# An MM-DiT attention block on one core: the shift-times-V rows beside the text scale rows, and the text gate rows beside the text output, each as one tiled run, with the text adds on GpSimd

## Chip, cores, metric

One core of one Trainium2 chip. The metric is the device time of one execution in microseconds (us); medians of several runs are quoted. The "span" in a profile is from the first to the last instruction of one profiled execution, about 2 us less than the time. Runs carry a state, fast or slow; verdicts use fast runs.

## The reference

```python
B, Ni, Nt, D = (2, 256, 32, 1152)          # all bfloat16
mod_i = (silu(c) @ wmod_img).reshape(B, 6, 1, D);  mod_t = (silu(c) @ wmod_txt).reshape(B, 6, 1, D)
shi, sci, gai = mod_i[:, 0], mod_i[:, 1], mod_i[:, 2];  sht, sct, gat = mod_t[:, 0], mod_t[:, 1], mod_t[:, 2]
hi = layernorm(x_img) * (1 + sci) + shi;   ht = layernorm(x_txt) * (1 + sct) + sht
qkvi = hi @ wqkv_img;                      qkvt = ht @ wqkv_txt      # D -> 3D each
q, k, v = concat(text, image)              # 288 tokens per batch
a = softmax(q @ k.T * D**-0.5) @ v
out_i = x_img + gai * (a_img @ wo_img);    out_t = x_txt + gat * (a_txt @ wo_txt)
```

Nearly 40 MB of weights are read once each, in blocks of 1152 x 1152 (2.65 MB).

## The kernel before

Weights pass through five buffers ("slots"). A load into a slot is issued by SyncE, in program order, and can be issued only when everything that reads the slot's old weights is done:

```python
def load_w(slot, src, c0, splits=(D,)):        # one block into one slot, queue of SyncE
    t = wtile(slot)
    ...
        nc.sync.dma_start(t[:, :, o:o + n], sv[:, :, o:o + n])
...
w_k_i = load_w(4, wqkv_img, D)
w_sc_t = load_w(1, wmod_txt, D)
w_q_t = load_w(2, wqkv_txt, 0)
```

Small products with few rows run on "tiled" TensorE: four independent strips of 32 columns. These are the modulation rows (`gps` in the profile):

```python
def mod_rows_of(w, lhs):
    gps = ps_tr.tile([P, KT, LW], f32, tag="tr")
    for kt in range(KT):
        for g in range(NGG):                   # NGG = 4 strips
            mm(gps[LW * g:LW * g + LW], lhsT=lhs[:, kt, :], rhs=group(w, kt, g),
               start=(kt == 0), stop=(kt == KT - 1), tile_position=(0, LW * g))
    return gps
```

The image part does not apply the shift to its values directly: the product of shift and V weights is added later, as a row. For the text values that row has to be copied to 32 partitions, so it goes out to memory and is read back:

```python
def shift_v_rows():
    p_sv = mod_rows_of(w_v_i, shT32)
    nc.scalar.copy(svr[:], p_sv[:])
    cols["v"] = mod_cols_of(p_sv, "svc")
    for b in range(B):                         # the write, queue of ScalarE
        nc.scalar.dma_start(svd[b].rearrange("(c g l) -> g c l", g=NGG, l=LW), svr[b:P:LW])
    for g in range(2):                         # the read-back, queue of SyncE
        for b in range(B):
            r0 = 64 * g + NT * b
            nc.sync.dma_start(svb[r0:r0 + NT, :], svd[b, g * HD:(g + 1) * HD].partition_broadcast(NT))
...
v_last()
shift_v_rows()                                 # before the first q matmul
w_k_t = load_w(3, wqkv_txt, D)
w_ga_i = load_w(0, wmod_img, 2 * D)
w_v_t = load_w(1, wqkv_txt, 2 * D)
w_o_i = load_rows(4, wo_img, 0)
...
```

At the end the text gate takes a similar way through memory (`mod_scratch`, then `gbf`), and the text output stands after the third of four image tiles:

```python
out_img(0, C3)
out_img(1, C3, between=txt_gate)
out_img(2, C3)
out_txt()                                      # 64-column strips; product and add on VectorE
out_img(3, (CH, CH, 224, 160), parts=(2 * CH, D - 160, D))
```

Of the kernel before, what the change touches and what calls it, by code (L numbers as in the profile page):

```python
# [14 lines left out]
def kernel(  # L15
# [14 lines left out]
    nc = tc.nc  # L30
    bf = mybir.dt.bfloat16
    f32 = mybir.dt.float32
    PSUM = bass.MemoryType.PSUM

    B, NI, D = x_img.shape
    NT = x_txt.shape[1]
    P = 128
    KT = D // P
# [3 lines left out]
    NTT = B * NT  # L42
    CH = 384
    NCH = D // CH
    VC = 288
# [9 lines left out]
    ps_mm = ctx.enter_context(tc.tile_pool(name="ps_mm", bufs=6, space=PSUM))  # L55
    ps_tr = ctx.enter_context(tc.tile_pool(name="ps_tr", bufs=2, space=PSUM))

    pin = tc.keep_in_program_order

    def mm(*a, **k):  # L60
        return pin(nc.tensor.matmul(*a, **k))  # L61

    def tr(*a, **k):
        return pin(nc.tensor.transpose(*a, **k))  # L64
# [6 lines left out]
    x_i = act.tile([P, NIT, D], bf)  # L71
# [4 lines left out]
    def wtile(slot):  # L76
        return wpool.tile([P, KT, D], bf, tag="w%d" % slot, name="t")
# [6 lines left out]
    def load_w(slot, src, c0, splits=(D,)):  # L84
        t = wtile(slot)
        sv = wview(src, c0)
        o = 0
        for n in splits:
            nc.sync.dma_start(t[:, :, o:o + n], sv[:, :, o:o + n])
            o += n  # L90
        return t

    def load_rows(slot, src, c0, cuts=(0, 3, 6)):
        t = wtile(slot)
        sv = wview(src, c0)
        for r0, r1 in zip(cuts, cuts[1:] + (KT,)):
            nc.sync.dma_start(t[:, r0:r1, :], sv[:, r0:r1, :])
        return t
# [14 lines left out]
    w_sh_t = load_rows(0, wmod_txt, 0, (0, 1, 3, 6))  # L113
    nc.sync.dma_start(x_t[:], xt_flat[:, :])
    w_k_i = load_w(4, wqkv_img, D)
    w_sc_t = load_w(1, wmod_txt, D)
    w_q_t = load_w(2, wqkv_txt, 0)

    nc.scalar.preload_act_table_set("natural_log_exp_and_others")
    eps_t = eps_row[:, 0:1]  # L120
# [197 lines left out]
    t3, t0, t6 = [(x_tiles(k0, 1), k0, 1) for k0 in (3, 0, 6)]  # L318
# [63 lines left out]
    def qk_img(wq, blk, hooks):  # L382
        for j in range(KT):
            for hook in hooks.get(j, ()):
                hook()
            ps = ps_mm.tile([P, B * NI], f32, tag="mm")
            for kt in range(KT):
                mm(ps[:], lhsT=wq[:, kt, j * P:(j + 1) * P], rhs=hT_i[:, kt, :],
                   start=(kt == 0), stop=(kt == KT - 1))
            qk_evac(qkT[:, blk * KT + j, :, 0:NI], ps[:].rearrange("p (b n) -> p b n", b=B), blk)  # L390
# [4 lines left out]
    v_t = act.tile([P, HD + NTT], bf)  # L395
# [4 lines left out]
# [6 lines that stand above are left out]
        for g in range(2):  # L406
# [3 lines that stand above are left out]
# [84 lines left out]
    def qk_txt(blk, wq):  # L494
        for j0 in range(0, KT, FG):
            jn = min(FG, KT - j0)
            ps = ps_mm.tile([P, FG, NTT], f32, tag="mm")
            for j in range(j0, j0 + jn):
                for kt in range(KT):
                    mm(ps[:, j - j0, :], lhsT=wq[:, kt, j * P:(j + 1) * P], rhs=hT_t[:, kt, :],  # L500
                       start=(kt == 0), stop=(kt == KT - 1))
            qk_evac(qkT[:, blk * KT + j0:blk * KT + j0 + jn, :, NI:NTOK],
                    ps[:, 0:jn, :].rearrange("p j (b n) -> p j b n", b=B), blk)
# [11 lines left out]
    def v_txt_out(r, ps):  # L515
        pin(nc.vector.tensor_sub(v_t[:, r * VC:(r + 1) * VC], ps[:], svb[:, r * VC:(r + 1) * VC]))
        if r == 0:
            pin(nc.vector.tensor_sub(v_t[0:NTT, HD:HD + NTT], ps[NTT:P, 0:NTT], svb[NTT:P, 0:NTT]))
# [20 lines left out]
    gb = act.tile([P, B, D], bf, tag="Bt")  # L539
    gbf = act.tile([P, 2, VC], bf)  # L540
    xf = act.tile([P, 2, VC], bf)
# [14 lines left out]
    def txt_gate():  # L556
        mod_row_out(mod_rows(w_ga_t), 1)
        for g in range(2):
            for b in range(B):
                r0 = 64 * g + 32 * b  # L560
                nc.gpsimd.dma_start(gbf[r0:r0 + NT, :, :],
                                    gsc[1, b, :].rearrange("(r g j) -> g r j", r=2, g=2)[g].partition_broadcast(NT))

    v_last()
    shift_v_rows()
    w_k_t = load_w(3, wqkv_txt, D)
    w_ga_i = load_w(0, wmod_img, 2 * D)
    w_v_t = load_w(1, wqkv_txt, 2 * D)
    w_o_i = load_rows(4, wo_img, 0)
    w_ga_t = load_w(3, wmod_txt, 2 * D)  # L570
    w_o_t = load_rows(1, wo_txt, 0, (0, 5))
    qk_img(w_q_i, 0, {0: (shift_part(0, 2),), 3: (txt_stats, shift_part(2, 4), txt_var, txt_norm),
                      5: (shift_part(4, 7),), 8: (shift_part(7, KT),)})
    qk_img(w_k_i, 1, {1: (txt_transposes,), 4: (txt_rows_scale, shift_blocks, txt_scale),
                      7: (shift_fold, txt_shift), 8: (lambda: qk_txt(0, w_q_t),)})
    qk_txt(1, w_k_t)

    aT = act.tile([P, KT, B * NTOK], bf, tag="Q")
    qpos = [[0, P, 2 * P], [NT, NT + P, 0]]
# [50 lines left out]
    def p_transposes(kj, pool):  # L630
        ps = pool.tile([P, B * NTOK], bf, tag="tr" if pool is ps_tr else "mm", name="pT_ps")
        k0 = kj * P
        for pb, c0, o in [(pbs[(0, qi)], k0, qpos[0][qi]) for qi in range(TPB)] + [(pbs["t"], k0, NI)] + \
                [(pbs[(1, qi)], k0 - (NT if kj == 2 else 0), NTOK + qpos[1][qi]) for qi in range(TPB)]:
            tr(ps[:, o:o + P], pb[:, c0:c0 + P], ident[:])
        return ps

    def p_out(kj, ps, copy, b0=0, b1=B):
        pin(copy(pT[:, kj, b0 * NTOK:b1 * NTOK], ps[:, b0 * NTOK:b1 * NTOK]))
# [55 lines left out]
    v_txt_out(0, vt[0])  # L695
    vt.append(v_txt(1))
    pt0, pt1, pt2 = p_transposes(0, ps_tr), p_transposes(1, ps_tr), p_transposes(2, ps_mm)
    v_txt_out(1, vt[1])
    p_out(0, pt0, nc.scalar.copy, 0, 1)
    p_out(0, pt0, nc.vector.tensor_copy, 1, B)  # L700
    p_out(1, pt1, nc.scalar.copy, 0, 1)
    p_out(2, pt2, nc.vector.tensor_copy)
    p_out(1, pt1, nc.scalar.copy, 1, B)
    img_gate_spread()
    for dts in ((0, 5, 1), (6, 2, 7), (3, 8, 4)):
        attn_pair(*[[(b, dt) for dt in dts] for b in range(B)])

    def out_img(i, chunks, parts=None, between=None):
        b = i // TPB
        t0 = b * NTOK + qpos[b][i % TPB]  # L710
        o = work.tile([P, D], bf, tag="o")
        c0 = s0 = 0
        for n in chunks:
            if c0 and between:
                between = between()
            ps = ps_mm.tile([P, CH], f32, tag="mm")
            for dt in range(KT):
                mm(ps[:, 0:n], lhsT=aT[:, dt, t0:t0 + P], rhs=w_o_i[:, dt, c0:c0 + n],
                   start=(dt == 0), stop=(dt == KT - 1))
            tmp = work.tile([P, CH], bf, tag="tmp")  # L720
            nc.vector.tensor_mul(tmp[:, 0:n], ps[:, 0:n], gb[:, b, c0:c0 + n])  # L721
            nc.vector.tensor_add(o[:, c0:c0 + n], tmp[:, 0:n], x_i[:, i, c0:c0 + n])  # L722
            c0 += n
            if parts is None and c0 == D or parts and c0 in parts:
                (nc.scalar if parts and c0 == D else nc.sync).dma_start(oi_v[b, i % TPB, :, s0:c0], o[:, s0:c0])
                s0 = c0

    def out_txt():
        of = work.tile([P, 2, VC], bf, tag="of", bufs=1)
        for r in range(2):  # L730
            ps = ps_mm.tile([P, VC], f32, tag="mm")
            for dt in range(KT):
                for g in range(2):
                    c0 = (2 * r + g) * VC
                    mm(ps[64 * g:64 * g + NTT, :], lhsT=aT[:, dt, NI:NI + NTT], rhs=w_o_t[:, dt, c0:c0 + VC],
                       start=(dt == 0), stop=(dt == KT - 1), tile_position=(0, 64 * g))
            tmp = work.tile([P, CH], bf, tag="tmp")
            nc.vector.tensor_mul(tmp[:, 0:VC], ps[:], gbf[:, r, :])
            nc.vector.tensor_add(of[:, r, :], tmp[:, 0:VC], xf[:, r, :])
        for g in range(2):  # L740
            eng = nc.sync if g == 0 else nc.scalar
            eng.dma_start(ot_flat.rearrange("t (r g j) -> g t r j", r=2, g=2)[g], of[64 * g:64 * g + NTT, :, :])

    C3 = (CH, CH, CH)
    out_img(0, C3)
    out_img(1, C3, between=txt_gate)
    out_img(2, C3)
    out_txt()
    out_img(3, (CH, CH, 224, 160), parts=(2 * CH, D - 160, D))


# [28 lines left out]
```

## Time and profile before

| | before |
|---|---|
| time, median of 6 runs | 117.75 us (117.37 to 118.41) |
| span of the profiled run | 115.7 us |
| TensorE busy | 95% |
| text v starts (first matmul that reads `hT_t` as weights) | 81.94 us |
| text output starts | 105.65 us |
| text output weights landed | 101.9 us |

In the page, a digit of a slice row is the busy share of a fortieth of the span in tenths; "GB/s" is what the DMA engines moved in it. In a timeline, the columns are start, duration, engine, line, operation, tiles, and in brackets how long the engine stood idle before and what ended that. "SPq" is SyncE's queue: the duration there is the time to issue a transfer, not to carry it out. The lines themselves are in the prediction below.

### The profile page before, as it was taken

What the parts mean: (1) busy time and instruction counts of PE and PEld (TensorE: products, weight loads), DVE (VectorE), ACT (ScalarE), POOL (GpSimd) and SP (SyncE); (2) the same over time, 40 slices, a digit from 0 to 9 for tenths busy, and PEclk for the clock granted to TensorE, in tenths of its full rate; (3) what the DMA queues carried; (4) which work ended last, traced back from release to release, by engine and by line L of the source; (5) the groups of instructions that cost most, each with busy time, mean ns of one, the idle gap of its engine ahead of it and who ended that gap; (6) DMA issues with size and microseconds to landing.
All of it is one profiled execution on the core that took longest, in us unless ns stands there. A gap on an engine that the chain in (4) does not pass through costs nothing.

```text
span 115.7 us, 2570 instructions
## 1 busy us (share of the span) xinstructions
PE 109.6 (95%) x1069; PEld 63.3 (55%) x1078; DVE 72.2 (62%) x152; ACT 43.9 (38%) x93; POOL 12.2 (11%) x32
## 2 busy tenths in 40 slices
PE   4998899999999999999999999999999999999990
PEld 2335644445584444445454458787866566557670
DVE  3469692053868999999996040018768508666671
ACT  4699810042652289825330324244647400100000
POOL 7200000000000000000000000002450700434000
PEclk9999999999999999999999999999999999999998
DMA  3999999999999999999999999999999999942223
GB/s 97 366 378 404 408 406 409 413 410 413 409 403 410 320 387 408 407 410 414 412 363 395 411 404 413 413 409 406 413 404 410 404 421 374 386 167 51 102 51 102
DMA packets 18917, 41.02 MB, mean 355 GB/s; under 512 B 1323, under 2 KB 1851, under 8 KB 18907
## 3 DMA queue, kind: packets, MB, share of 16 engines
q1 hardware_dynamic: 18032, 39.85, 89.7%
q0 software_dynamic: 480, 0.89, 2.2%
q10 hardware_dynamic: 395, 0.12, 0.4%
q8 instruction: 8, 0.13, 0.4%
q14 instruction: 2, 0.02, 0.0%
HBM read 39.52 MB, written 1.34 MB: 353 GB/s over the span
## 4 chain that ended last, share of the span: by engine, by line
PE 84%; ACT 5%; DVE 4%; DMA 3%; issue 1%; DVEq 0%
PE ps L61 52%; PE vps L61 15%; PE gps L61 5%; PE aps L61 5%; PE sps L61 4%; DMA x_i<-in_x_img_dram 3%; ACT xn_i L194 2%; ACT xn_i L195 2%; DVE tmp L721 1%; DVE xT_i L257 1%; PE pT_ps L64 1%; DVE o L722 1%; PE tp L64 1%; PE sc_ps L61 1%; DVE xn_i L209 0%
## 5 line engine op out<-in xcount | busy, mean ns | idle before, releaser
L61 PE MATMUL ps<-xT_i,t 128*128 128x512 bf16 x157 | 35.4, 379 | 0.3
L61 PEld LDWEIGHTS <-t 128*128 128x128 bf16 x333 | 21.0, 98 | 19.1 <-issue 0.7
L450 DVE SCALAR_TENSOR_TENSOR acc_sh<-t,sTf,acc_sh 128x1152 f32<-128x1152 bf16 x16 | 21.4, 1409 | 0.0
L61 PE MATMUL ps<-t,aT 128*128 128x384 bf16 (+3 forms) x153 | 20.3, 308 | 0.0
L61 PE MATMUL vps<-t,hS_i 128*128 128x512 bf16 (+1 forms) x105 | 17.7, 324 | 0.3 <-DVE hS_i L269 0.2
L61 PEld LDWEIGHTS <-aT 128*128 128x128 bf16 (+1 forms) x153 | 13.0, 101 | 7.1 <-issue 0.8
L61 PEld LDWEIGHTS <-hS_i 128*128 128x128 bf16 x108 | 9.0, 98 | 8.9 <-DVE hS_i L269 0.4
L721 DVE TENSOR_TENSOR tmp<-ps,gb 128x384 bf16<-128x384 f32 (+2 forms) x13 | 6.8, 524 | 7.9 <-DMA gb<-mod_scratch 4.0
L380 ACT CAST qkT<-ps 128x512 bf16<-128x512 f32 (+2 forms) x11 | 6.1, 552 | 14.8 <-PE ps L61 13.5
L607 POOL TENSOR_SCALAR pb<-e,rs 128x32 bf16<-128x32 f32 (+1 forms) x5 | 2.3, 459 | 75.9 <-DVE rs L599 75.9
L378 ACT ACTIVATE qkT<-ps 128x512 bf16<-128x512 f32 (+2 forms) x11 | 6.0, 560 | 8.3 <-PE ps L61 6.7
L61 PE MATMUL wps<-warm 128*128 128x512 bf16 x23 | 7.3, 472 | 1.5 <-DVE unit L127 1.5
L177 DVE CAST v_i<-vps 128x512 bf16<-128x512 f32 x5 | 3.5, 692 | 8.0 <-PE vps L61 8.0
L587 DVE TENSOR_REDUCE nmx<-sps 128x1 f32<-128x288 f32 x4 | 1.8, 458 | 9.4 <-PE sps L61 9.4
L179 ACT CAST v_i<-vps 128x512 bf16<-128x512 f32 x4 | 2.3, 581 | 10.1 <-PE vps L61 10.1
L61 PEld LDWEIGHTS <-sT 128*32 128x32 bf16 x180 | 4.5, 96 | 1.8 <-issue 1.2
L61 PE MATMUL sps<-qkT 128*128 128x288 bf16 (+1 forms) x54 | 5.3, 287 | 0.0
L652 DVE TENSOR_SCALAR aT<-aps,svc 128x288 bf16<-128x288 f32 x9 | 4.3, 518 | 1.5 <-PE aps L61 1.5
L61 PE MATMUL gps<-t,sT 128*32 128x288 bf16 x144 | 5.2, 287 | 0.0
L61 PEld LDWEIGHTS <-warm 128*128 128x128 bf16 x25 | 2.6, 112 | 4.9 <-issue 2.1
L61 PE MATMUL aps<-pT,v_i 128*128 128x288 bf16 x36 | 5.1, 287 | 0.0
L61 PE MATMUL ps<-hT_t,t 128*128 128x64 bf16 x162 | 5.1, 193 | 0.0
(112 smaller groups left out, 104.7 us busy)
## 6 DMA issues: line engine op xcount, KB each, us to landing
t<-in_wqkv_txt_dram SPq DMA_DIRECT2D x3, 2592.0 KB, 19.1
t<-in_wmod_img_dram SPq DMA_DIRECT2D x2, 2592.0 KB, 13.8
t<-in_wmod_txt_dram SPq DMA_DIRECT2D x2, 2592.0 KB, 18.4
t<-in_wqkv_img_dram SPq DMA_DIRECT2D x3, 864.0 KB, 13.6
t<-in_wqkv_img_dram SPq DMA_DIRECT2D x1, 2592.0 KB
t<-in_wo_img_dram SPq DMA_DIRECT2D x3, 864.0 KB, 9.9
t<-in_wqkv_img_dram SPq DMA_DIRECT2D x3, 576.0 KB, 10.0
t<-in_wmod_txt_dram SPq DMA_DIRECT2D x2, 864.0 KB, 13.4
```

Of the source, the lines that this page charges most:

```text
L61: return pin(nc.tensor.matmul(*a, **k))
L64: return pin(nc.tensor.transpose(*a, **k))
L177: nc.vector.tensor_copy(out_ap, in_ap)
L179: nc.scalar.copy(out_ap, in_ap)
L194: pin(nc.scalar.activation(junk, x_ap, ACT.Copy, scale=1.0 / D, accum_out=sm[:, 0:1]))
L195: pin(nc.scalar.activation(junk, x_ap, ACT.Square, scale=float(D) ** -0.5, accum_out=sm[:, 1:2]))
L378: nc.scalar.mul(out_ap, in_ap, SCALE)
L380: nc.scalar.copy(out_ap, in_ap)
L450: pin(nc.vector.scalar_tensor_tensor(acc, w_sh_t[:, kt, :], col, acc, op0=ALU.mult, op1=ALU.add))
L607: pin(nc.gpsimd.tensor_scalar(dst, src, rs[0:qn, :], 0.0, op0=ALU.mult, op1=ALU.add))
L652: nc.vector.tensor_scalar(dst, tiles[(b, dt)][:], bias, None, op0=ALU.add)
L721: nc.vector.tensor_mul(tmp[:, 0:n], ps[:, 0:n], gb[:, b, c0:c0 + n])
```

## The change

Each change between tilings of TensorE costs about 0.095 us (read from the trace of the kernel before, in the prediction), so two pairs of tiled runs are joined: the shift-times-V rows with the text scale rows (in the third block of the k phase), and the text gate rows with the text output, both on 32-column strips. As the image V weights are then read until later, the slots are dealt out anew. VectorE is spared the two text adds. The diff, with its smaller hunks cut:

```diff
@@ -113,8 +113,9 @@
-    w_sc_t = load_w(1, wmod_txt, D)
-    w_q_t = load_w(2, wqkv_txt, 0)
+    w_sc_t = load_w(2, wmod_txt, D)
+    w_q_t = load_w(3, wqkv_txt, 0)
+    w_k_t = load_w(1, wqkv_txt, D)
@@ -562,18 +563,21 @@
     v_last()
-    shift_v_rows()
-    w_k_t = load_w(3, wqkv_txt, D)
-    w_ga_i = load_w(0, wmod_img, 2 * D)
-    w_v_t = load_w(1, wqkv_txt, 2 * D)
-    w_o_i = load_rows(4, wo_img, 0)
-    w_ga_t = load_w(3, wmod_txt, 2 * D)
-    w_o_t = load_rows(1, wo_txt, 0, (0, 5))
+    late = {}
+
+    def late_loads():
+        late["ga_i"] = load_w(0, wmod_img, 2 * D)
+        late["v_t"] = load_w(2, wqkv_txt, 2 * D)
+        late["o_i"] = load_rows(4, wo_img, 0)
+        late["ga_t"] = load_w(3, wmod_txt, 2 * D)
+        late["o_t"] = load_rows(1, wo_txt, 0, (0, 7))
 ...
-    qk_img(w_k_i, 1, {1: (txt_transposes,), 4: (txt_rows_scale, shift_blocks, txt_scale),
+    qk_img(w_k_i, 1, {1: (txt_transposes,), 3: (shift_v_rows, txt_rows_scale, late_loads, shift_blocks, txt_scale),
                       7: (shift_fold, txt_shift), 8: (lambda: qk_txt(0, w_q_t),)})
@@ -695,57 +699,63 @@
+    p_out(0, pt0, nc.vector.tensor_copy, 0, 1)
     v_txt_out(1, vt[1])
-    p_out(0, pt0, nc.scalar.copy, 0, 1)
-    p_out(0, pt0, nc.vector.tensor_copy, 1, B)
     p_out(1, pt1, nc.scalar.copy, 0, 1)
+    p_out(0, pt0, nc.scalar.copy, 1, B)
 ... (out_txt: 32-column strips, rows 0 to 6 of the weights first, then 7 and 8)
+    def out_txt_store(tiles):
         of = work.tile([P, 2, VC], bf, tag="of", bufs=1)
+        for r, ps in enumerate(tiles):
             tmp = work.tile([P, CH], bf, tag="tmp")
-            nc.vector.tensor_mul(tmp[:, 0:VC], ps[:], gbf[:, r, :])
-            nc.vector.tensor_add(of[:, r, :], tmp[:, 0:VC], xf[:, r, :])
+            pin(nc.vector.tensor_mul(tmp[:, 0:VC], ps[:], gbf[:, r, :]))
+            pin(nc.gpsimd.tensor_add(of[:, r, :], tmp[:, 0:VC], xf[:, r, :]))
 ...
     out_img(0, C3)
-    out_img(1, C3, between=txt_gate)
+    out_img(1, C3)
+    txt_gate()
+    txt = out_txt()
     out_img(2, C3)
-    out_txt()
+    out_txt_store(txt)
     out_img(3, (CH, CH, 224, 160), parts=(2 * CH, D - 160, D))
```

More of the change, by code (lines that the diff above doesn't have):

```diff
@@ L564 @@
     v_last()
-    shift_v_rows()
-    w_k_t = load_w(3, wqkv_txt, D)
-    w_ga_i = load_w(0, wmod_img, 2 * D)
-    w_v_t = load_w(1, wqkv_txt, 2 * D)
-    w_o_i = load_rows(4, wo_img, 0)
-    w_ga_t = load_w(3, wmod_txt, 2 * D)
-    w_o_t = load_rows(1, wo_txt, 0, (0, 5))
+    late = {}
[5 more added lines that the diff above has]
+        late["o_t"] = load_rows(1, wo_txt, 0, (0, 7))
     qk_img(w_q_i, 0, {0: (shift_part(0, 2),), 3: (txt_stats, shift_part(2, 4), txt_var, txt_norm),
                       5: (shift_part(4, 7),), 8: (shift_part(7, KT),)})
-    qk_img(w_k_i, 1, {1: (txt_transposes,), 4: (txt_rows_scale, shift_blocks, txt_scale),
+    qk_img(w_k_i, 1, {1: (txt_transposes,), 3: (shift_v_rows, txt_rows_scale, late_loads, shift_blocks, txt_scale),
                       7: (shift_fold, txt_shift), 8: (lambda: qk_txt(0, w_q_t),)})
     qk_txt(1, w_k_t)
+    w_ga_i, w_v_t, w_o_i, w_ga_t, w_o_t = [late[k] for k in ("ga_i", "v_t", "o_i", "ga_t", "o_t")]
     aT = act.tile([P, KT, B * NTOK], bf, tag="Q")
@@ L706, with out_img @@
         attn_pair(*[[(b, dt) for dt in dts] for b in range(B)])
-    def out_img(i, chunks, parts=None, between=None):
+    def out_img(i, chunks, parts=None):
         b = i // TPB
@@ L713, in out_img @@
         for n in chunks:
-            if c0 and between:
-                between = between()
             ps = ps_mm.tile([P, CH], f32, tag="mm")
@@ L720, in out_img @@
             tmp = work.tile([P, CH], bf, tag="tmp")
-            nc.vector.tensor_mul(tmp[:, 0:n], ps[:, 0:n], gb[:, b, c0:c0 + n])
-            nc.vector.tensor_add(o[:, c0:c0 + n], tmp[:, 0:n], x_i[:, i, c0:c0 + n])
+            pin(nc.vector.tensor_mul(tmp[:, 0:n], ps[:, 0:n], gb[:, b, c0:c0 + n]))
+            pin(nc.vector.tensor_add(o[:, c0:c0 + n], tmp[:, 0:n], x_i[:, i, c0:c0 + n]))
             c0 += n
@@ L728, in out_txt @@
     def out_txt():
-        of = work.tile([P, 2, VC], bf, tag="of", bufs=1)
-        for r in range(2):
-            ps = ps_mm.tile([P, VC], f32, tag="mm")
-            for dt in range(KT):
-                for g in range(2):
-                    c0 = (2 * r + g) * VC
-                    mm(ps[64 * g:64 * g + NTT, :], lhsT=aT[:, dt, NI:NI + NTT], rhs=w_o_t[:, dt, c0:c0 + VC],
-                       start=(dt == 0), stop=(dt == KT - 1), tile_position=(0, 64 * g))
+        tiles = [ps_tr.tile([P, VC], f32, tag="tr", name="txo") for r in range(2)]
+        for d0, d1 in ((0, 7), (7, KT)):
+            for r, ps in enumerate(tiles):
+                for dt in range(d0, d1):
+                    for g in range(2):
+                        for b in range(B):
+                            c0, r0, t0 = (2 * r + g) * VC, 64 * g + NT * b, NI + NT * b
+                            mm(ps[r0:r0 + NT, :], lhsT=aT[:, dt, t0:t0 + NT], rhs=w_o_t[:, dt, c0:c0 + VC],
+                               start=(dt == 0), stop=(dt == KT - 1), tile_position=(0, r0))
+        return tiles
+    def out_txt_store(tiles):
+        of = work.tile([P, 2, VC], bf, tag="of", bufs=1)
+        for r, ps in enumerate(tiles):
             tmp = work.tile([P, CH], bf, tag="tmp")
-            nc.vector.tensor_mul(tmp[:, 0:VC], ps[:], gbf[:, r, :])
-            nc.vector.tensor_add(of[:, r, :], tmp[:, 0:VC], xf[:, r, :])
+            pin(nc.vector.tensor_mul(tmp[:, 0:VC], ps[:], gbf[:, r, :]))
+            pin(nc.gpsimd.tensor_add(of[:, r, :], tmp[:, 0:VC], xf[:, r, :]))
         for g in range(2):
```

## The prediction

> **What bounds the kernel now.** I read the page's engine shares first, then its 40 slices, then the chain of work that ended last, and after that the timeline at the places which the change touches.
>
> ```profile
> PE 109.6 (95%) x1069; PEld 63.3 (55%) x1078; DVE 72.2 (62%) x152; ACT 43.9 (38%) x93; POOL 12.2 (11%) x32
> ...
> PE   4998899999999999999999999999999999999990
> ...
> DMA  3999999999999999999999999999999999942223
> ...
> PE 84%; ACT 5%; DVE 4%; DMA 3%; issue 1%; DVEq 0%
> ```
>
> Two things are full at once. TensorE is busy in every slice after the start and makes 84% of the chain, at a clock of 0.995. The DMA engines are full as well until slice 34 of 40 (about 100 us); 41 MB at the 410 GB/s of those slices needs 100 us. Weights stream through five slots in an order fixed by the program, so TensorE lives on a few microseconds of lead.
>
> TensorE's own idle places are small. The timeline of TensorE around the text scale rows, from two narrow windows:
>
> ```profile
> 59.35 0.81 PE L61 MATMUL ps<-xT_i,t 128*128 128x512 bf16 x3
> 60.09 0.55 PE L61 MATMUL gps<-t,sT 128*32 128x288 bf16 x12
> ```
> ```profile
> 60.72 0.66 PE L61 MATMUL gps<-t,sT 128*32 128x288 bf16 x15
> 61.31 0.39 PE L61 MATMUL ps<-xT_i,t 128*128 128x512 bf16 x1
> ```
>
> Columns are start, duration, engine, line, operation. One 128x512 matmul lasts 0.379 us but the next starts sooner: (0.81 - 0.38) / 2 = 0.216 us apart. The last of the three therefore starts at 59.78, and the first matmul on 32-column tiles at 60.09, 0.31 later, which is 0.09 more than the pace. At the way out, the last gps starts at 60.72 + 0.66 - 0.29 = 61.09, the next full matmul at 61.31: 0.22 against a pace of 0.12 for four tiled matmuls ((1.29 - 0.29) / 8 for a run of 36). So each change of tiling costs about 0.095 us, a tiled run costs two.
>
> The end of the kernel, from the timeline of all engines (ps is the output projection, gbf the text gate broadcast back from memory):
>
> ```profile
> 97.01 1.29 PE L61 MATMUL gps<-t,sT 128*32 128x288 bf16 x36
> ...
> 98.35 0.40 ACT L535 CAST g_sb<-gps 128x288 bf16<-128x288 f32 x1 [6.76 <-PE gps L61]
> ...
> 99.04 1.22 POOL L537 DMA_DIRECT2D mod_scratch<-g_sb  x2 [7.16 <-ACT g_sb L535]
> ...
> 103.19 2.17 POOL L561 DMA_DIRECT2D gbf<-mod_scratch  x4 [2.93 <-DMA mod_scratch<-g_sb]
> ...
> 107.05 0.46 DVE L738 TENSOR_TENSOR tmp<-ps,gbf 128x288 bf16<-128x288 f32 x1 [0.35 <-PE ps L61]
> ...
> 112.60 0.32 DVE L721 TENSOR_TENSOR tmp<-ps,gb 128x160 bf16<-128x160 f32 x1
> 112.95 0.24 DVE L722 TENSOR_TENSOR o<-tmp,x_i 128x160 bf16<-128x160 bf16 x1
> ```
>
> The gate takes a long way: rows on TensorE until 98.2, a cast, a write to memory that lands 3 to 4 us after its issue, then four reads of which the last is issued at 104.8 and, by the view of the tile gbf, lands 2.1 us later, at 106.9. From the end of the gate rows that is 8.7 us. VectorE needs it only at 107.05, and there its wait was ended by TensorE: the gate was just in time. The last VectorE add ends at 113.2 and the last store closes the span.
>
> Last, the text output weights (tile view):
>
> ```profile
> L97 SPq DMA_DIRECT2D t<-in_wo_txt_dram x2: 368/560/752, 84.5 to 84.9; - x2
> ...
> DMA to landing us min/median/max: 17.0/17.0/17.0
> ```
>
> The second part is issued at 84.9 and lands at 101.9; its matmuls start at 105.65. Lead: 3.7 us.
>
> **What the Trainium skill says.** "TensorEngine Tiling (Array Packing)", Tiling Modes, Key Properties: changing the tiling mode, not just the tile, drains TensorE. The trace agrees, with the 0.09 to 0.10 us above. "GPSIMD Engine Reference", section 3.1: a two-input add costs GpSimd about 2.6 cycles per element at 1.2 GHz, measured there in fp32, plus dispatch. Estimate for 288 columns: 288 x 2.6 / 1.2 = 0.62 us plus some 0.2, so 0.8 to 0.9 us; VectorE's add of that size took 0.31 here. No GpSimd add is in this trace. "SBUF — State Buffer", Who interferes with whom: a VectorE operation with two SBUF inputs contends with GpSimd's reads; the residual adds are of that kind. No place here shows it. "DMA: Bandwidth & Descriptors", Issuing engines are not separate DMA queues: all queues share the same 16 engines. The trace agrees in its long write latencies while the weight stream runs (4.0 us from issue to landing at 99, against 2.1 for the reads at 104).
>
> **The change part by part.**
>
> 1. Rows beside rows. The shift-times-V rows leave the place before the first q matmul, and join the text scale rows one block earlier in the k phase. One way in and one out vanish: 2 x 0.095 = 0.19 us of TensorE. The rows themselves (1.1 us) only move. The text gate rows leave the middle of the second image output tile and stand directly before the text output, which goes from 64-column to 32-column tiles, so both have one tiling. Its 36 matmuls become 72, in four tiles instead of two: still 18 rounds of 0.12 us. Another 0.19 us, and the slow first round of the 64-column form (0.143 against 0.122) goes: 0.02. Sum on TensorE: 0.4 us, all on the path, because TensorE is back to back.
>
> 2. Slots. Text scale weights, text q and text k go to slots 2, 3 and 1 instead of 1, 2 and 3. Text q used to be issued at 37.8; now it waits until the image q weights are done. The q phase starts 1.3 us earlier than before (34.45 - 1.1 - 0.2 = 33.15), lasts 81 x 0.216 = 17.5, ends at 50.65. The stream then still has the text scale weights to deliver until about 52.4 (19.9 MB counted along the stream), and the first load of the kernel shows about 1.0 us from issue to first packet, so hardly a hole: 0.2 us. Text k waits for the shift-times-V rows: 50.65 + 3 x 1.95 + 0.4 + 1.1 = 58.0, data from about 59.3; text q is through at 59.0: a hole of 0.4. The gate weights come after the four svb reads in SyncE's order, and these wait for a write issued only at 58.6: a hole of 0 to 0.6. Together the weight stream slips by 0.5 to 1.2 us. Before, the text v weights landed at 80.5 (issue 61.4 + 19.1) with use at 81.9, so they still just fit (use at 81.75).
>
> 3. Text output moved up by one image tile. It starts after six chunks: 91.07 - 0.19 + 6 x 1.462 + 1.2 = 100.85, where it was 105.65. The first seven rows of its weights are 78% of 2.65 MB; the rest takes 0.59 MB / 0.41 = 1.4 us. With the last byte at 101.9 + 0.5 to 1.2, the first part lands at 101.0 to 101.7: a new TensorE wait of 0.2 to 0.9 us, centre 0.5. The last two rows are needed 14 rounds (1.7 us) later and come about then. This eats the 0.4 us of part 1.
>
> 4. Gate later, use after tile 2. The gate rows end 2 x 1.462 - 0.19 = 2.7 us later, at 100.95. With the same 8.7 us way the gate lands at 109.65; the weight stream has ended by then, so the write may be a microsecond faster: 108.8 to 109.6. VectorE is free from image tile 2 at 91.07 - 0.19 + 6 x 1.462 + 3.45 + 4.39 + 0.5 = 108.0, plus 1.0 for its last chunk: 109.0. So the gate costs 0 to 0.6 us of waiting, centre t = 109.3.
>
> 5. GpSimd adds. VectorE saves 2 x 0.31. But tmp has two buffers: the first chunk of image tile 3 can be multiplied only when GpSimd has read the first text product (t + 0.5 + 0.85 = 1.4), the second chunk after the second (t + 2.3). Then VectorE's tail: 0.95 + 0.95 + 0.6 + 0.55 = 3.0, so the last add ends at about t + 4.5 = 113.8, against 113.2 now.
>
> 6. The order of the copies of the transposed probabilities: one goes ahead of the text v subtraction on VectorE. TensorE waits only 0.1 us there now (the tiling change); I book zero.
>
> **The rivals.**
> A, the arithmetic of TensorE alone: only the four tiling changes count, 117.76 - 0.4 = 117.35. For it: no TensorE gap but those in the middle of the kernel. Against it: both moved pieces lose their lead.
> B, the weight stream: text output waits for its weights; end = 113.2 - 0.4 + 0.5 = 113.3, time 117.85; with a slip of 2 us 119.
> C, gate latency and VectorE's tail (parts 4 and 5): 113.8, time 118.35. For it: the gate already had only a few tenths of spare time. Against: the write may land quicker once the stream is over.
> B and C run side by side, so the later one counts, not their sum. A wait in B of over 1 us hides C.
> D, the text v weights arrive late too and everything behind shifts: some tenths more.
>
> **Range and chances.** Between A at 117.35 and C at 118.35, with B in between, I put 118.0. The low end 117.2 is A with nothing lost; the high end 119.2 is a slip of over 2 us in the stream or VectorE blocked by GpSimd. Faster by 2% would be below 115.4, which no part offers: 0.01. Slower by 2% would be above 120.1, a stream slip of 3 us: 0.05. Within 2%: 0.94.
>
> **What would show it.** In the changed timeline: two tiled runs of 72 (rows) and 108 (gate plus output) with no full-width matmul inside, and four fewer 0.095 us steps. Part 2: slices of lower GB/s near 52, 59 and 65 us. Part 3: a TensorE wait on the text output weights at about 101; if there is none, B is wrong. Part 4: VectorE's first text product waiting for gbf rather than TensorE, near 109. Part 5: GpSimd adds of 0.8 to 0.9 us, and VectorE's third image tile waiting on POOL. If the last TensorE matmul still releases the last product, C is wrong and the time is near 117.4.

## The result, and the profile after

The changed kernel takes 121.67 us (median of 6, 120.88 to 122.45) against 117.75 us: ratio 1.033, 95% interval 1.027 to 1.039, slower. (Ratios here are the mean time of one kernel's fast runs over that of the other's fast runs of the same rounds, so not quite the ratio of the medians. Executions over 1.5% slower than the fastest of the same kernel are left out of the means.) It is above the predicted range.

The page after, with the lines that answer to those of before:

```profile
PE 109.2 (92%) x1105; PEld 63.4 (53%) x1114; DVE 71.6 (60%) x150; ACT 43.6 (37%) x93; POOL 13.6 (11%) x34
...
PE   5988999999999999999999999995699999889990
...
DMA  3999999999999999999989689999999999950133
GB/s 96 385 395 383 396 402 411 412 413 412 410 401 385 321 412 408 414 333 409 399 303 401 237 255 410 410 409 411 403 410 410 415 373 412 411 214 17 33 128 119
...
PE 50%; DMA 39%; DVE 4%; SPq 3%; issue 1%; POOL 1%; DVEq 0%
```

TensorE is busy for as long as before, and the share of DMA in the chain has gone from 3% to 39%. In the row of DMA rates, slices 22 and 23, counted from 0 (65.5 to 71.5 us), fall to 237 and 255 GB/s: the weight stream has a hole there. In TensorE's row two slices are thin, near 83 and near 104 us. The timeline of TensorE names what it waited for (from two windows):

```profile
84.53 2.39 PE L61 MATMUL ps<-t,hT_t 128*32 128x288 bf16 x72 [2.48 <-DMA t<-in_wqkv_txt_dram]
```
```profile
104.57 2.39 PE L61 MATMUL txo<-t,aT 128*32 128x288 bf16 x72 [0.92 <-DMA t<-in_wo_txt_dram]
```

Text v starts 2.6 us late, because its weights are not there, and the text output another 1.1 us late. (The brackets count from the modelled end of the last matmul, from start to start the excess over the pace is 2.64 and 1.08 us.) Counted along TensorE: -0.2 us for two tiling changes less in the k phase, +2.64, +1.08, -0.2 for the tail, sum +3.3. The last matmul starts 3.30 us later than before (115.63 against 112.33), and the span is 3.4 us longer. So the waits for weights are the whole loss of this profiled run. At 120.88 us it is the fastest of the six, and the medians differ by 3.9 us; point 5 below comes back to the rest.

Why were the weights late? SyncE's queue between 45 and 69 us, before and after:

```profile
45.01 7.65 SPq L409 DMA_DIRECT2D svb<-sv_scratch  x4
52.76 0.39 SPq L89 DMA_DIRECT2D t<-in_wqkv_txt_dram  x1
58.34 0.39 SPq L89 DMA_DIRECT2D t<-in_wmod_img_dram  x1
61.42 3.72 SPq L89 DMA_DIRECT2D t<-in_wqkv_txt_dram  x1
```
```profile
50.87 7.71 SPq L89 DMA_DIRECT2D t<-in_wqkv_txt_dram  x2
64.64 3.01 SPq L410 DMA_DIRECT2D svb<-sv_scratch  x4
67.75 0.39 SPq L89 DMA_DIRECT2D t<-in_wmod_img_dram  x1
68.18 0.67 SPq L89 DMA_DIRECT2D t<-in_wqkv_txt_dram  x1
```

Before, the read-back (svb) was issued at 45 to 52.7 us, behind loads that kept the engines supplied. After, SyncE issues the text k load at 58.2 and then stands until 64.6. Its own waits say for what:

```profile
SPq L410 <- DMA sv_scratch<-svr: 6.5, 2, 6.0
```

For the write of the shift-times-V rows, issued by ScalarE at 58.65 and 59.31. Then the four reads take 3.0 us to issue, and only at 67.75 comes the next big load (the image gate), 9.4 us later than before. The text k data had been through at about 67. One stretch in two kernels, first after, then before (busy time of each engine, then TensorE's clock, DMA share and GB/s at the end of the line):

```profile
66.00:70.00 4.00, 4.00 (x52) 2.35 (x50) 1.22 (x3) 1.17 (x2) 0.00 (x0) 1.00 0.62 169
```
```profile
66.00:70.00 4.00, 4.00 (x47) 2.28 (x45) 1.22 (x3) 1.17 (x2) 0.00 (x0) 1.00 1.04 408
```

4 us at 169 instead of 408 GB/s is 2.3 us of stream lost. By the bytes counted along the stream it ends at 104.2 us instead of 100.7: a slip of 3.5 us, of which the rates give 2.3 to this hole, 0.6 to one at 52 to 54 us (text q's slot) and some 0.3 net to 58 to 62 (text k's slot). The remaining 0.3 is about what the read-back itself carries (0.15 MB, counted in the 169 GB/s but no part of the weights). The trace shows one thing more. Of the 16 packets of 4 bytes that end text v's load (completion marks, as I read them), 15 come at 82.5 to 82.9 us and one at 84.1; before, the 16 were spread from 78.2 to 80.2. So the last mark slipped by 3.9 us, 0.4 more than the bytes.

**Theory:** the joined rows bring the write and the read-back of the shift-times-V rows to a place where they stand in SyncE's queue ahead of the next big load, and the stream runs dry behind them. **Rival 1:** the slots that come free later (the holes at 52 and 58 us) are what counts. **Rival 2:** the tail costs it: gate used too late, text output moved up, GpSimd adds.

### The profile page after: what moved, and what is told of

Its sections match the earlier page's. It is cut to its first block, busy times and chain, and to the rows that moved or that the text cites. A ratio compares the mean times of both kernels' runs of the same rounds, so it can differ in the third digit from the quotient of the medians.

```text
span 119.1 us, 2642 instructions
## 1 busy us (share of the span) xinstructions
PE 109.2 (92%) x1105; PEld 63.4 (53%) x1114; DVE 71.6 (60%) x150; ACT 43.6 (37%) x93; POOL 13.6 (11%) x34
## 4 chain that ended last, share of the span: by engine, by line
PE 50%; DMA 39%; DVE 4%; SPq 3%; issue 1%; POOL 1%; DVEq 0%
PE ps L61 30%; DMA t<-in_wo_txt_dram 19%; PE vps L61 15%; DMA t<-in_wqkv_txt_dram 12%; DMA t<-in_wqkv_img_dram 8%; PE gps L61 3%; SPq L108 2%; PE txo L61 2%; DVE tmp L723 2%; DVE o L724 1%; SPq L104 1%; POOL of L747 1%; DVE tmp L746 0%; SPq L89 0%; PE tpt L64 0%
## 5 line engine op out<-in xcount | busy, mean ns | idle before, releaser
L61 PE MATMUL ps<-t,aT 128*128 128x384 bf16 (+2 forms) x117 | 17.9, 314 | 0.0
```

The source lines that it names most:

```text
L61: return pin(nc.tensor.matmul(*a, **k))
```

## The experiments

All outputs are right. "Before" was run beside each set on the same chip; its median was 117.71, 117.83 and 117.80 us in the three sets.

### The two halves alone: e2_tail_only, e3_front_only

e2 is the kernel before with the last diff hunk and the cut of the text output weights at row 7; e3 is the kernel before with the first two hunks (cut at row 5 as before).

> The kernel before, with only the tail of the change: text gate rows directly before the text output on 32-column tiles, GpSimd adds, the copy order, and the text output weights cut at row 7. Theory (the weight stream's slip does the damage, the tail is about neutral): no wait before text v; text output weights land at about 102 as before, first part near 100.6 against a need at about 100.9; time 117.4 to 118.4. Rival 2 (tail costs it): 120 or more. My recorded sum for the gate's way plus VectorE's tail says +0.6, so 118.3.

Measured: 117.53 us (117.30 to 118.85), ratio 1.002 (0.995 to 1.008). The tail alone costs nothing. Rival 2 is out for the loss as a whole.

> The kernel before, with only the front of the change: the slots, shift-times-V rows beside the text scale rows, late loads after them. Theory: the hole of 66 to 70 stays, TensorE waits 2.5 to 3 us before text v, text output weights land near 106 and are needed at 108, so no second wait: time 117.75 - 0.2 + 2.7 = 119.8 to 120.8. Rival 2 (tail costs it): about 117.6 to 118.3.

Measured: 122.77 us (121.83 to 124.65), ratio 1.040 (1.033 to 1.047); the fast runs are 121.83, 122.19 and 123.36; the profiled run, 124.65, counts as slow. The front carries the loss, but this is more than I had expected. The profile of the slow run points to a second cost (window view of 80 to 86 and 86 to 91 us; the value after the last bracket is TensorE's clock):

```profile
80.00:86.00 6.00, 1.91 (x55) 1.41 (x54) 2.75 (x9) 2.06 (x8) 2.83 (x6) 0.92 1.04 409
86.00:91.00 5.00, 4.44 (x73) 2.65 (x73) 0.69 (x2) 0.00 (x0) 1.54 (x3) 0.50 1.04 408
```
```profile
86.56 4.51 PE L61 MATMUL ps<-t,hT_t 128*32 128x288 bf16 x72 [4.64 <-DMA t<-in_wqkv_txt_dram]
```

TensorE stood for 4.6 us, and then its clock was 0.50: the 72 matmuls of text v took 4.5 us instead of 2.4. Its three fast runs have mean clocks of 0.984 to 0.986, so by these means each had a stretch at a lower clock too. The Trainium skill's "TensorE: Matmul & The Clock Gate", Part 1, What's actually happening, describes this: a clock gate passes half the pulses after an idle window of about 3.4 us. The trace agrees: 0.50 after a wait of 4.6 us, while the clock of the changed kernel's profile stays at 1.00 from 82 to 92 us, through its wait of 2.5. That the wait itself was 4.6 us here and 2.5 in the full change is not explained by the hole: by the bytes, text v's load was through at 82.2 in this run and at 82.7 in the other. In the trace's records of 4-byte packets (completion marks, as I read them) nearly all of a group of 16 come at 81.8 to 82.5 in this run, so one DMA engine was far behind. Why, I leave open.

### The write alone: f4_write_late_alone

The kernel before, with TensorE's program, slots and tail untouched. Only the write and read-back are issued later, and the loads behind them as a group (the diff is abridged):

```diff
-    (write and read-back inside shift_v_rows, before q)
+    def shift_v_io():   # the same two loops; the writes pinned in ScalarE's order
...
-    qk_img(w_k_i, 1, {1: (txt_transposes,), 4: (txt_rows_scale, shift_blocks, txt_scale),
+    qk_img(w_k_i, 1, {1: (txt_transposes,), 3: (shift_v_io,), 4: (txt_rows_scale, late_loads, shift_blocks, txt_scale),
```

> The kernel before, in which one thing is changed: the two writes of the shift-times-V rows to memory and their four reads back are issued late (after the third block of the k phase, near 58.9 us, as in the changed kernel) in front of the image gate load; TensorE's program, the slots and the tail are those of before. Theory (it is this write and read-back in front of the gate load in SyncE's order that opens the hole): gate load issued near 67.5 us, a hole of 2 to 3 us in the weight stream at 66 to 70, text v weights land near 83.5, TensorE waits 1.5 to 2.5 us before text v, text output weights still in time; time 119.2 to 120.4, or up to 122 where the wait lets the TensorE clock fall. Rival 1 (late slots are what counts): within 0.3% of before.

Measured: 119.62 us (118.92 to 119.92), ratio 1.014 (1.010 to 1.018). SyncE's queue, its wait and TensorE's wait:

```profile
52.05 0.37 SPq L89 DMA_DIRECT2D t<-in_wqkv_txt_dram  x1
63.37 2.87 SPq L411 DMA_DIRECT2D svb<-sv_scratch  x4
66.33 0.39 SPq L89 DMA_DIRECT2D t<-in_wmod_img_dram  x1
```
```profile
SPq L411 <- DMA sv_scratch<-svr: 11.4, 2, 10.9
```
```profile
PEld L61 <- DMA t<-in_wqkv_txt_dram: 1.1, 1, 1.1
```

Moving nothing but these transfers makes the hole (265 and 95 GB/s in the two stretches 64 to 66 and 66 to 68 us), makes text v wait and costs 1.8 us: the interval is clear of 1. The profiled run is the fastest of the four; its span is 1.2 us longer than that of before, and text v's wait, which I had expected at 1.5 to 2.5 us, is 1.1 of it. The theory holds, and rival 1 is not needed for this part. The hole alone costs less than in the full change, where the stream had slipped by 0.6 us before it and text v is needed 0.2 us sooner.

### Taking the read-back out of SyncE's way: e4_readback_late, e1_readback_gpsimd

The full change, with the read-back moved behind two big loads (e4), or issued by GpSimd (e1):

```diff
 # e4, in late_loads
         late["v_t"] = load_w(2, wqkv_txt, 2 * D)
+        shift_v_reads()                 # the four reads, moved here from shift_v_rows
 # e1
-                nc.sync.dma_start(svb[r0:r0 + NT, :], svd[...])
+                nc.gpsimd.dma_start(svb[r0:r0 + NT, :], svd[...])
```

> The changed kernel, with the svb reads still on SyncE but after the image gate and text v loads, so that only the order in SyncE's queue differs. Theory: as with the reads on GpSimd: hole of 66 to 70 gone, time 117.6 to 118.6; svb now lands behind the text v weights near 82, about when text v is done, so up to 0.5 us more than there is possible. Rival 1: above 119.5.

Measured: 119.39 and 120.50 us, and two slow runs of 121.94 and 122.63; ratio of the two fast ones 1.019 (1.012 to 1.025), unclear, and above what was expected. The profiled run is the one of 119.39. Its window and waits:

```profile
66.00:70.00 4.00, 4.00 (x56) 2.47 (x55) 1.22 (x3) 1.17 (x2) 0.00 (x0) 1.00 1.03 386
```
```profile
PE txo L61 <- DMA t<-in_wo_txt_dram: 1.2, 1, 1.2
PEld L61 <- DMA t<-in_wqkv_txt_dram: 0.8, 1, 0.8
```

The gate load is issued at 58.6, and the hole at 66 to 70 is gone (386 GB/s). The wait before text v falls from 2.64 to 0.65 us, as expected. The wait for the text output weights stays at 1.4, which was not.

> The changed kernel, with the four reads of the shift-times-V rows back from memory (svb) issued by GpSimd instead of SyncE, so that the image gate load behind them no longer waits for the write. Theory (the hole of 66 to 70 us in the weight stream, 2.4 us by its rate, comes from SyncE standing at svb until 64.6 us and then issuing four reads until 67.7): the gate load is issued within a microsecond of 59, the hole goes, the text v weights land near 82 instead of 84.5, TensorE's wait before text v shrinks from 2.7 us to under 0.5, the wait for text output weights (1.1 us) goes too, and the time is 117.6 to 118.6. Rival 1 (the late release of slots 3 and 1, with holes near 52 and 59 us, is what counts): the hole near 66 goes but time stays above 119.5. Rival 2 (the gate at the end and the GpSimd adds cost it): no more than 1 us is won.

Measured: fast runs of 118.72, 119.08 and 120.00 us (the profiled run, 123.05, is slow), ratio 1.013 (1.007 to 1.019). That is 2% won of the full change's 3.3%, on another chip, and less than was expected. The only profile of e1 is that of the slow run (text v waits 1.35 us in it), so I use the one of e4. There the stream still ends 1.7 us behind that of before: 0.4 come from the hole at 52 us, 0.5 from the rates after it (356 to 392 GB/s between 60 and 70 us), and 0.8 between 80 and 84 us (351 and 387 GB/s), where the moved read-back is carried. So rival 1 may have a share: I put the rest of the loss, 1.3 to 1.9%, to the slots at first, and tested that next.

### Rows one block earlier: f3_rows_block2, f1_block2_gpsimd, f2_front_block2_gpsimd

```diff
-    qk_img(w_k_i, 1, {1: (txt_transposes,), 3: (shift_v_rows, txt_rows_scale, late_loads, shift_blocks, txt_scale),
+    qk_img(w_k_i, 1, {1: (txt_transposes,), 2: (shift_v_rows, txt_rows_scale, late_loads, shift_blocks, txt_scale),
```

f3 is the full change with this line; f1 also has the read-back on GpSimd; f2 is f1 with the tail of the kernel before.

> The changed kernel with the joined rows one block earlier (after the second k block, not the third), so that write, read-back and the text k load all start 1.95 us earlier; still all on SyncE. Theory (the hole at 66 to 70 lasts from the end of text k's data until the gate load's issue plus about 1 us): write issued near 56.7, gate load near 65.8, text k's data end near 66, so the hole shrinks from 2.4 to 0.5 to 1 us, text v lands 2 to 2.5 us earlier than in the changed kernel; time 118.0 to 119.3. Rival 1 (text q's and the slots' late release): text q's hole near 52 stays, only 0.4 us won: 120.5 to 121.5.

Measured: 118.22 us in the only fast run; 120.00, 120.22 and 120.84 are counted as slow, though their spans (117.3 to 117.8 us against 116.1) differ by less. What f3 takes as a rule stays open. The profile of the fast run answers the question asked, though: in SyncE's queue the whole sequence is 2 to 3 us earlier,

```profile
62.41 2.23 SPq L410 DMA_DIRECT2D svb<-sv_scratch  x4
64.74 0.39 SPq L89 DMA_DIRECT2D t<-in_wmod_img_dram  x1
```
```profile
66.00:70.00 4.00, 3.95 (x53) 2.44 (x53) 1.22 (x3) 1.17 (x2) 0.00 (x0) 1.00 0.99 346
```

and 66 to 70 is at 346 GB/s, a hole of 0.6 us where there had been 2.3. Text v does not wait; the text output waits 0.9 us for its weights. The hole follows the gate load's issue, as the theory says.

> The changed kernel with the rows one block earlier and the read-back issued by GpSimd. Theory: no hole at 58 to 62 nor at 66 to 70, that at 52 (0.5 us) stays; the stream ends 0.5 to 1 us behind that of before, so TensorE waits 0 to 0.8 us at the text output and not before text v; time 117.3 to 118.3. If it is above 119, a cause is still missing.

Measured: 118.40 us (118.04 to 118.56), ratio 1.004 (1.001 to 1.007). Just above what was expected. There is no hole left at 56 to 62 (409 GB/s), text v does not wait, and the text output waits 0.3 us for its weights.

> As the run before, with the tail of the kernel before (text output after the third image tile). Theory: text output weights are in time by 3 us, so only 0.2 us of tilings are won: 117.4 to 117.7, steady from run to run. If the loss sits in the tail after all, this is faster than the one before by more than the stream's slip.

Measured: 117.44 us (117.38 to 117.56), ratio 0.997 (0.994 to 0.999). The front, freed of the holes at 58 and at 66 us, gains what its tilings promised: from the first v matmul to the first score matmul 61.33 us against 61.55 before, 0.22 less. Its queue shows the difference to the full change, the gate load at 57.6 instead of 67.8, and GpSimd, idle otherwise, bears the wait:

```profile
57.64 0.37 SPq L89 DMA_DIRECT2D t<-in_wmod_img_dram  x1
```
```profile
62.96 2.14 POOL L410 DMA_DIRECT2D svb<-sv_scratch  x4 [57.18 <-DMA sv_scratch<-svr]
```

### Is the half clock a cost of its own? g1_front_keep_busy

The front-only kernel with 14 useless matmuls in the place of the wait (the trace below has lost the record of one):

```diff
     img_gate()
+    fill = ps_tr.tile([P, 512], f32, tag="tr", name="fill")
+    for _ in range(14):
+        mm(fill[:], lhsT=warm[:, 0:P], rhs=warm[:], start=True, stop=True)
     vt = [v_txt(0)]
```

> The front-only kernel, with 14 idle 128x512 matmuls (3.0 us at 0.216 each, into a spare PSUM tile that nobody reads) put just before text v, where TensorE otherwise waits 2.7 to 4.8 us. They can only delay text v, to 84.7 us at the earliest; they do no useful work. Theory (a wait of some microseconds also lets the TensorE clock fall to half, which the profile of the front-only kernel shows for 6.8 us, and this is the second part of its loss and of its spread): no stretch of half clock in the profile, mean clock above 0.99, times closer together, and 120.3 to 121.8 us, below the 121.8 to 124.7 of the front-only kernel, in spite of the added work. If the clock has no part: same as front-only or slower.

Measured: 120.81 us (120.60 to 121.02), ratio 1.026 (1.024 to 1.028), mean clocks 0.999 to 1.000 in all four runs. The same window as in front-only:

```profile
86.00:91.00 5.00, 5.00 (x87) 3.52 (x81) 3.25 (x8) 2.29 (x6) 1.92 (x4) 1.00 1.04 409
```
```profile
82.04 2.97 PE L61 MATMUL fill<-warm 128*128 128x512 bf16 x13 [0.16 <-issue]
84.94 2.39 PE L61 MATMUL ps<-t,hT_t 128*32 128x288 bf16 x72
```

More work, and less time by some 1.4% of the ratio, with a spread of 0.4 us instead of 1.5 in fast runs. The hole at 66 to 70 is as deep as before (199 GB/s), so the load was not what got better. The two were on different chips, which is why I compare ratios. (In this run text v's load had come by 84.9, in the profiled run of front-only only at 86.5: part of that run's loss is the late engine, not the clock.)

### The tail in detail: g3_tail_only_again, g2_tail_adds_on_vector

> Tail-only once more, with more rounds: theory -0.2 us of TensorE (two tilings and one slow round), partly lost to the later gate at VectorE: 117.3 to 117.8, ratio 0.996 to 1.000.

Measured: 117.87 us (117.58 to 118.39), ratio 1.001 (0.999 to 1.004), just above what was expected. The timelines of VectorE and GpSimd in e2_tail_only, then one line of VectorE in g3:

```profile
108.57 0.81 DVE L742 TENSOR_TENSOR tmp<-txo,gbf 128x288 bf16<-128x288 f32 x2
109.87 0.56 DVE L719 TENSOR_TENSOR tmp<-ps,gb 128x384 bf16<-128x384 f32 x1 [0.48 <-POOL of L743]
```
```profile
104.68 2.16 POOL L561 DMA_DIRECT2D gbf<-mod_scratch  x4 [1.80 <-DMA mod_scratch<-g_sb]
109.11 1.42 POOL L743 TENSOR_TENSOR of<-tmp,xf 128x288 bf16<-128x288 bf16 x2 [2.26 <-DVE tmp L742]
```
```profile
109.19 0.82 DVE L742 TENSOR_TENSOR tmp<-txo,gbf 128x288 bf16<-128x288 f32 x2 [0.50 <-DMA gbf<-mod_scratch]
```

In the profile of g3, TensorE's last matmul starts at 111.88, 0.45 earlier than in the kernel before, but the gate lands at 109.07 and VectorE's last add ends at 113.43, 0.23 later. In this profile the gain on TensorE is given back at VectorE, which waited 0.50 us for the gate.

The other run is e2 with `nc.vector.tensor_add` in place of `nc.gpsimd.tensor_add`.

> The tail-only kernel, with the two text adds back on VectorE. By the trace of tail-only the GpSimd adds last 0.71 and hold VectorE up by 0.48 us once, against 2 x 0.31 of VectorE work saved. So I expect a difference of under 0.2 us from tail-only: 117.3 to 117.8.

Measured: 118.04 us (117.62 to 118.89), ratio 1.003 (1.000 to 1.005). Not to be told from tail-only. In e2 the first chunk of the last image tile starts 1.30 us after the first text product (109.87 - 108.57), here 1.42 (110.39 - 108.97): the GpSimd adds gain 0.1 us there.

### The best version once more: g4_best_again

f2 in five rounds.

> The best version so far once more (rows one block earlier, read-back on GpSimd, tail of the kernel before): -0.2 us or a little more, ratio 0.995 to 0.999, steady.

Measured: 117.43 us (117.32 to 117.93), ratio 0.998 (0.996 to 0.9995). It beats both kernels, by 0.2 to 0.3% over before.

## Why the prediction was wrong, point by point

1. Part 1, four tiling changes less: right. 0.22 us in the front (f2), and about as much on TensorE in the tail (g3, allowing for a start that was 0.19 earlier).
2. Part 2, the slots: **this is the step that failed.** Its third term, "a hole of 0 to 0.6" behind the read-back, measured 2.3 us. I had the mechanism (reads in SyncE's order, waiting for a write issued at 58.6), but not the size, for which the prediction shows no working. By its own numbers text k's data (2.65 MB at 410 GB/s, from 59.3) end near 65.8. With 1.0 us from issue to data, a hole of at most 0.6 leaves the write and the reads until about 65.4, which is 6.8 us from 58.6. They took 9.1 us (58.65 to 67.75): the write held SyncE until 64.64, 5.3 us after the second issue, and the four reads took 3.0 us more to issue. Nor was the stream back 1.0 us after the gate load's issue (the prediction took that from issue to first packet of the kernel's first load): it moved 161 GB/s from 69.5 to 70.0 us and 364 in the next half, some 2.5 us after it. The first term (text q's slot) measured 0.6 instead of 0.2, with the full rate back as late after the issue at 50.87 (318 GB/s from 53.0 to 53.5, then 387); the second (text k's slot) about 0.3 net instead of 0.4. By the prediction's own sums these two would be 0 and 0.3. The slip was 3.5 us, not 0.5 to 1.2. The trace of before held a warning: by the view of the tile g_sb, the four writes of the gate rows, each as small as these (2.3 KB), landed 3.4 to 5.0 us after their issue.
3. "They still just fit" for the text v weights followed from that slip, so it fell too: 2.64 us of waiting in the changed kernel. f4 shows that the late write and read-back alone bring a wait there (1.1 us). With the read-back behind the loads (e4) it is 0.65 us, with the rows one block earlier (f3) none.
4. Part 3, the wait for text output weights: named, centre 0.5 us, measured 1.08. It was not larger because the wait at text v had already pushed the need back.
5. A cost that no step had: after a long wait TensorE can run at half clock (4.6 us in the profile of front-only). Of the changed kernel's six runs two had mean clocks of 0.982 and 0.980, at 122.17 and 122.45 us, and three of the four others lay at 120.9 to 121.2. One at 122.38 had 0.996, so not all of the spread is this. These runs were not profiled, so how long they waited is not known, and what half clock takes of the changed kernel's loss is not shown. g1 shows the cost in the front-only kernel.
6. Parts 4 and 5, gate and GpSimd: the mechanism was right (in g3 VectorE waited 0.50 us for the gate, then 0.49 for GpSimd; in the changed kernel only the second is left) and the size too large. A GpSimd add lasted about 0.7 us (two in 1.42), not 0.8 to 0.9, and in the two profiles of tail-only the last add ended at 112.8 and 113.4 us, not 113.8. Tail-only is neutral where I had said +0.6. (The gate rows end at 98.3 by the line in the prediction, 97.01 + 1.29, and not at 98.2; it changes nothing.)
7. Rival D, text v late, "some tenths more", was the main effect; B, with "a slip of 2 us 119", was the right family with too small a slip. A chance of 0.05 for slower was too low for a stream without slack whose slip I had only estimated: the prediction itself puts "slower" at a slip of 3 us.

What stays open: how the remaining 1.3 to 1.9% of e1 and e4 divide between the holes at 52 and 58 us, the rates after them and, in e4, the moved read-back (f1 takes away the hole at 58 and most of the loss together, but it also moves the write and the reads), and why one DMA engine was late in front-only.

## What to carry to other kernels

When a piece of work moves, look at every transfer that moves with it and at what stands behind it in the issuing engine's queue: a small write and read-back of some kilobytes cost more here than the whole move could gain, because the next 2.65 MB load stood behind it. Where a stream has no slack, put waits of that kind on a queue with nothing else to do (GpSimd here), and issue them early. And count a long TensorE wait as dearer than its length: half clock followed the one of 4.6 us here, though not the one of 2.5 us in the changed kernel's profile.

## What the Trainium skill lacked or had wrong

- "DMA: Bandwidth & Descriptors", Latency and other measured facts: it speaks of about 2 us of fixed cost per DMA. A write of some kilobytes to memory while big loads were queued released its waiter 5.3 us after the second issue (64.64 - 59.31), and the first of its reads could only then be issued. No page gives a time for a small transfer beside a full stream.
- "TensorEngine Tiling (Array Packing)", Key Properties: it says that a change of tiling mode drains TensorE, not how much that costs. Here 0.09 to 0.10 us each, and 0.22 us won by two fewer (f2).
- "GPSIMD Engine Reference", section 3.1: its figure is for fp32. A bfloat16 add of 128x288 took about 0.7 us, close to the 0.62 us plus dispatch that the prediction estimated from it.
